# Widening of all MLP weights beside the expert tiles, and three pieces of them split there

## The chip, the cores and the metric

The kernel runs on one core of a Trainium2 chip. The metric is the device time of one execution in microseconds; before the change the median of three runs is 971.08 us (969.3 to 971.67).

## The reference, cut to what matters

Three layers follow each other on 2304 tokens (4 batches of 576) of 512 columns:

```python
# 1. attention per batch and head (D = 64), mixed with a memory read-out by a gate g
out = g * mem_out + (1 - g) * softmax(causal(q @ k.T / 8)) @ v
# 2. a mixture of 8 experts, one per token
e = argmax(x @ w_gate);  p = softmax(x @ w_gate)[e]
x = p * (relu(x @ w1[e]) @ w2[e])             # w1: 512 x 1024, w2: 1024 x 512
# 3. an MLP with an ELU, 512 -> 2048 -> 512
h = x @ w_in
y = where(h > 0, h, exp(min(h, 0)) - 1) @ w_out
```

`w_in` and `w_out` reach the kernel as 64-bit floats, all else as 32-bit floats.

## The kernel before, in words

**Matmuls.** A product of two float32 matrices is made of three passes of 128 x 128 x 512 in a reduced 32-bit format: each operand is split into a high part (a cast) and a low part (the operand less its high part), and high x high, low x high and high x low are added in PSUM. So each weight needs one cast (ScalarE or VectorE) and one subtraction (VectorE or GpSimd) before its first use; `split` records both.

**Stages.** Attention runs in pairs of heads. Then come 23 expert tiles of 128 tokens (tile 0 to 22), sorted by expert; two more tiles stand behind a branch that all engines take on a count made on the chip (`tc.If(nt > NTM)`), and are skipped when 23 suffice, as here. A tile loads its expert's weights (2 x 2 MB) only if the expert differs from the tile before, and splits them only then, in eight quarters: `w0` to `w3` (first matrix) and `w4` to `w7` (second). Even tiles load into `wraw`, odd ones into `wrbw`. A tile's second product is summed in one PSUM bank, `pm7`, which all tiles share, and evacuated from there into `y`.

**The MLP** takes the tokens in groups of 512 in the order of the expert tiles. A group has 16 units: 12 matmuls per 512 tokens for 128 columns of `w_in` (`h`), the ELU (ScalarE: `elu`, `tnh`; VectorE: three instructions), the split of the result (`gh`, `gl`), and 12 matmuls with `w_out`. The first group's tokens come from the first four tiles: two stay on the chip (`raw1n`), two are read back from `ye`; the tokens of later groups are scattered to `yd` and read from there.

**Its weights** are cut into 16 pieces of 512 KB, piece n = 2s + k: part k (0 `w_in`, 1 `w_out`) of slice s. Two things happen to a piece. *Widening* (class `Widen`) turns 64-bit words into 32-bit floats with integer operations, in two parts of 512 columns: a load of 512 KB into one of two buffers `wide`, one `Abs` on ScalarE, four VectorE instructions in `half`, and a store of 256 KB to `wf` in DRAM. Pieces 0 to 11 (24 parts) are widened beside the expert tiles. *Splitting* comes later: the piece is loaded back from `wf` and split into its place. Piece 0 is split beside the tiles; pieces 1 to 11 are loaded through `half`, `half1` and `wide` and split in the MLP's own program (`weights`); pieces 12 to 15 are widened there as well and split straight away. `raw0n` is piece 0, `wraw1n`, `wraw2n`, `wraw3n` are pieces 1 to 3 (each lies over one of tile 22's buffers of raw weights, `wraw1` to `wraw3`), `w02` is piece 4, `w12` piece 5, `w03` piece 6.

**The order of the work** is made ahead of time: class `Plan` takes every operation with a cost, a priority and its reads and writes, simulates the engines, and emits them in order of their planned start. Each engine runs its own list strictly in that order, and so does SP, which issues nearly all loads and stores: an instruction that waits holds all behind it. An operation may name two engines, and the planner gives it to the one that is done first by its costs. Some operations of the MLP's plan (in the old program the splits of pieces 1 and 2, and loads into `wide` and `half`) stand ahead of the branch in the engines' lists.

Of the kernel before, what the change touches and what calls it, by code (L numbers as in the profile page):

```python
# [9 lines left out]
F32 = mybir.dt.float32  # L10
F32R = mybir.dt.float32r
# [7 lines left out]
P = 128  # L19
# [17 lines left out]
NY = 2  # L37
YW = NY * P

NS = 6  # L40
assert NE <= -(-((B - 1) * S - E * (P - 1)) // P)
BIG = 1.0e30
LATE = 25000.0
# [40 lines left out]
class Plan:  # L84
# [137 lines left out]


KNOBS = {
    "xe": ("ACT", "DVE"), "he": ("ACT",), "re": [("ACT",), ("ACT", "DVE")], "m_ld": 4000.0, "m_x": -2208.9, "m_1": -1447.9, "m_h": -4434.5,
    "m_lag": 0.0, "m_if": 700.0, "m_fl": -3000.0, "m_wl": 300.0, "wa": 0, "wa0": 10022.449169040721, "wa1": 23927.854833523612, "wt": 1, "wp": 16, "wj": 2000.0,
    "m_g": -500, "wq": 0.85, "sa": 60.0, "sm": 50.0, "s2": 0.0, "step": -68438.62, "hd": -241.62,
    "mem": 379947.52, "xg": 4,
    "wh": [("ACT", "DVE"), ("ACT", "DVE"), ("ACT", "DVE"), ("DVE",), ("ACT",), ("ACT", "DVE"), ("ACT", "DVE"), ("ACT", "DVE")],
    "wl": [("DVE",)] * 8, "ord": [3, 4, 2, 1, 0], "rings": 4, "ab": 2, "nq": 2, "nv": 2, "na": 2, "na4": 2, "nx": 2, "nls": 2, "wide": 1, "de": ("DVE", "POOL"),  # L230
# [224 lines left out]
def cv(n):  # L455
    return 70 + 1.04 * n
# [10 lines left out]
def cpt(n):  # L467
    return 150 + 2.1 * n
# [615 lines left out]
class Widen:  # L1084
# [3 lines left out]
    N = 512  # L1088
# [11 lines left out]
    def inside(cls, tc, c, w_in, w_out):  # L1100
        return cls(tc, c, w_in, w_out, cls.ring(c), Ring("wo", [c.half[:, cls.N * i:cls.N * (i + 1)] for i in range(2)]))

    def part(self, n, pr, to=None, **kw):
        nc, c, pl, N = self.nc, self.c, self.c.pl, self.N
        ch, hf = divmod(n, 2)
        k, s = ch % 2, ch // 2
        sd = Slot(self.words)
        so = to or Slot(self.out)

        def o():  # L1110
            return so.t[:, N * hf:N * (hf + 1)] if to else so.t

        def u():
            return o().bitcast(U32)

        def f():
            if k == 0:
                nc.sync.dma_start(sd.t.rearrange("p (c f) w -> p c (f w)", c=2), self.vi[s, :, 2 * hf:2 * hf + 2].rearrange("p c f w -> p c (f w)"))
            else:
                nc.sync.dma_start(sd.t, self.vo[s, :, hf])  # L1120
        pl.op("SP", 480, f, w=[sd], prio=pr, dma=1456, lag=c.K["m_wl"], **kw)
        w = [(so, hf)]

        def f():
            nc.scalar.activation(o(), sd.t[:, :, 1].bitcast(F32), AF.Abs)
        pl.op("ACT", ca(N, sb=True), f, r=[sd], w=w, prio=pr)

        def f():
            nc.vector.tensor_scalar(o(), o(), 2.0 ** -15, MAXHI, op0=ALU.max, op1=ALU.min)  # L1129
        pl.op("DVE", cv2(N), f, w=w, prio=pr)  # L1130

        def f():
            nc.vector.tensor_scalar(u(), u(), 5, 2, op0=ALU.logical_shift_left, op1=ALU.logical_shift_right)  # L1133
        pl.op("DVE", cv2(N), f, w=w, prio=pr)

        def f():
            nc.vector.scalar_tensor_tensor(u(), sd.t[:, :, 0], 29, u(), op0=ALU.logical_shift_right, op1=ALU.bitwise_or)  # L1137
        pl.op("DVE", cv(N), f, r=[sd], w=w, prio=pr)

        def f():  # L1140
            nc.vector.scalar_tensor_tensor(u(), sd.t[:, :, 1], 0xC0000000, u(), op0=ALU.bitwise_and, op1=ALU.bitwise_or)  # L1141
        pl.op("DVE", cv(N), f, r=[sd], w=w, prio=pr)
        if to:
            return

        def f():
            nc.sync.dma_start(c.wf[ch, :, N * hf:N * (hf + 1)], o())
        pl.op("SP", 480, f, r=w, w=[], prio=pr, dma=728, lag=c.K["m_wl"])
# [75 lines left out]
def moe(tc, c, w1, w2, tiles):  # L1224
    nc = tc.nc
    mp, pl, K = c.mp, c.pl, c.K
# [201 lines left out]
        mtile(t)  # L1428
    if tiles[0] == 0:

        sr = Slot(c.wd.words)

        def src():
            return sr.t.rearrange("p n w -> p (n w)").bitcast(F32)

        def f():
            nc.sync.dma_start(src(), c.wf[0])
        pl.op("SP", 480, f, r=[("tile", K["wp"]), "y0"], w=[sr], prio=1.0e6, dma=1456)
        split(c, src, lambda: c.w0.t[:, 0], lambda: c.w0.t[:, 1], 1024, [sr], "w0h", "w0", 1.0e6, False, ("ACT", "DVE"), ("DVE", "POOL"))


def moe2(tc, c, w_in, w_out, out):
    nc = tc.nc
    tp, pl = c.tp, c.pl
# [19 lines left out]
    def chunk(t, cc, n):  # L1464
# [19 lines left out]
    def split(src, hi, lo, n, rd, wh, wl, pr, psum, also=()):  # L1484
        def ha():
            nc.scalar.copy(hi(), src())  # L1486

        def hv():
            nc.vector.tensor_copy(hi(), src())  # L1489

        def lv():
            nc.vector.tensor_sub(lo(), src(), hi().bitcast(F32))  # L1492

        def lp():
            nc.gpsimd.tensor_sub(lo(), src(), hi().bitcast(F32))  # L1495
        pl.op(("ACT", "DVE"), (ca(n, sb=not psum), cv(n) if psum else cv2(n)), (ha, hv), r=rd, w=[wh, *also], prio=pr)
        if psum:
            pl.op("DVE", cv(n), lv, r=rd + [wh], w=[wl], prio=pr)
        else:
            pl.op(("DVE", "POOL"), (cv(n), cpt(n)), (lv, lp), r=rd + [wh], w=[wl], prio=pr)  # L1500

    def weights(s):
        for k in range(2) if s else (1,):
            def mk(k):
                pr = 200.0 * s + 50 * k
                sr = Slot(r_raw) if s > 1 else Slot(wd.words)
                rd = [(sr, 0), (sr, 1)] + (["raw"] if s > 1 else [])

                def src():
                    return sr.t if s > 1 else sr.t.rearrange("p n w -> p (n w)").bitcast(F32)  # L1510

                def f():
                    nc.sync.dma_start(src(), c.wf[2 * s + k])
# [5 lines left out]
                split(src, lambda: wpart(k, 0, s), lambda: wpart(k, 1, s), 1024, rd, ("w", k, 0, s), ("w", k, 1, s), pr - 1000, False)
            mk(k)  # L1520

    for s in range(8):
        weights(s)
# [10 lines left out]
    def prep(g):  # L1534
        pr = start[g] - 900
# [120 lines left out]
def kernel(ctx, tc, q, k, v, M_prev, z_prev, beta, w_gate, w1, w2, w_in, w_out, out):  # L1656
    nc = tc.nc
# [126 lines left out]
```

## Time and profile before

| | |
|---|---|
| median of three runs | 971.08 us |
| the profiled execution | 969.31 us, span 967.6 us |
| TensorE busy / VectorE / ScalarE / GpSimd | 930.2 / 642.6 / 439.8 / 187.2 us |
| mean granted clock of TensorE | 0.989 |
| moved by DMA | 105.79 MB |

The stages in that span: attention to some 260 us, expert tiles to 542 us (a tile every 12.4 us), the MLP to the end. A line of a timeline gives the start, the busy time, the engine, the source line, the operation and its tiles (out<-in), and in square brackets the idle time of the engine just before it and what ended that.

### The profile page before, as it was taken

The page shows a single profiled execution, that of the slowest core. Times are in us where ns is not written, and L with a number is a line of the kernel's source. Part 1 is how long each engine was busy: PE and PEld are TensorE (multiplying, and loading weights), DVE is VectorE, ACT ScalarE, POOL GpSimd, SP SyncE. Part 2 cuts the span into 40 slices and gives each one's busy share as a digit, 9 for nine tenths or more (in the row PEclk, how much of TensorE's full clock was granted, in tenths as well). Part 3 has the DMA queues.
Part 4 walks back from the last instruction along what each step waited for, and adds up shares of the span by engine and source line. Part 5 has one row for each costly group of instructions (what it writes and reads, how often), then busy time and mean ns, then how long its engine had stood idle before and what let it go on. Part 6 is the DMA issues. An engine that isn't in the chain of part 4 may idle for free. (4 is left out here: it accounts for less than half of the span.)

```text
span 967.6 us, 18413 instructions
## 1 busy us (share of the span) xinstructions
PE 930.2 (96%) x6858; PEld 768.9 (79%) x6858; DVE 642.6 (66%) x1183; ACT 439.8 (45%) x893; POOL 187.2 (19%) x249
## 2 busy tenths in 40 slices
PE   9998999989999999999999898999999999999996
PEld 6777777777688888888887787888888888888895
DVE  3888878797865478438896499754565556555553
ACT  4777778865643357347665344222122212222221
POOL 3443443443200112212210113010001000100010
PEclk8999999999999999999999899999999999999998
DMA  6323334261814685398875434110011000100000
GB/s 122 87 65 102 74 75 112 57 211 58 297 48 139 218 282 196 103 306 327 299 272 197 153 123 125 45 44 1 1 44 44 1 12 23 44 0 1 12 33 22
DMA packets 94867, 105.79 MB, mean 109 GB/s; under 512 B 64687, under 2 KB 64687, under 8 KB 92465
## 3 DMA queue, kind: packets, MB, share of 16 engines
q1 hardware_dynamic: 88768, 91.06, 30.4%
q0 software_dynamic: 4800, 13.18, 3.8%
q8 instruction: 55, 0.90, 0.4%
q10 hardware_dynamic: 1200, 0.30, 0.2%
q14 instruction: 44, 0.35, 0.1%
HBM read 85.84 MB, written 21.31 MB: 111 GB/s over the span
## 5 line engine op out<-in xcount | busy, mean ns | idle before, releaser
L1598 ACT ACTIVATE elu<-pt 128x512 f32<-128x512 f32 x72 | 43.1, 599 | 253.9 <-PE pt L1590 253.8
L1623 PE MATMUL pt<-w,gh 128*128 128x512 f32 x432 | 135.5, 395 | 0.5 <-DVE gh L1489 0.5
L1380 PE MATMUL pm<-w,hh 128*128 128x512 f32 x368 | 128.3, 410 | 2.9 <-ACT y L1393 2.9
L1606 DVE TENSOR_SCALAR elu<-elu 128x512 f32<-128x512 f32 x72 | 30.6, 427 | 119.8 <-ACT elu L1598 119.8
L1623 PEld LDWEIGHTS pt<-w,gh 128*128 128x128 f32 x432 | 80.3, 190 | 17.3 <-DVE gh L1489 0.9
L1623 PE MATMUL pt<-w,gl 128*128 128x512 f32 x216 | 85.7, 397 | 3.0 <-POOL gl L1495 3.0
L690 ACT ACTIVATE a<-pat,st 128x128 f32<-128x128 f32 (+2 forms) x144 | 78.2, 552 | 22.5 <-DVE st L685 21.4
L1380 PEld LDWEIGHTS pm<-w,hh 128*128 128x128 f32 x368 | 70.6, 192 | 18.7 <-ACT y L1393 3.4
L1380 PE MATMUL pm<-w,hl 128*128 128x512 f32 x184 | 74.3, 404 | 0.3 <-DVE hl L1214 0.3
L685 DVE TENSOR_REDUCE st<-pat 128x2 f32<-128x256 f32 (+4 forms) x80 | 63.8, 807 | 9.0 <-PE pat L669 9.0
L1590 PE MATMUL pt<-yTh,w 128*128 128x256 f32 (+1 forms) x288 | 68.6, 318 | 0.0
L703 PE MATMUL pat<-ident,a 128*128 128x128 f32 x400 | 55.0, 280 | 9.1 <-ACT a L690 8.8
L626 POOL TENSOR_SCALAR ex<-ex 128x512 f32<-128x512 f32 (+1 forms) x32 | 37.9, 1184 | 128.8 <-ACT ex L602 118.1
L703 PEld LDWEIGHTS pat<-ident,a 128*128 128x128 f32 x400 | 42.9, 141 | 16.8 <-ACT a L690 15.7
L1610 DVE SCALAR_TENSOR_TENSOR tnh<-tnh,elu 128x512 f32<-128x512 f32 x72 | 49.6, 690 | 5.8
L1337 PE MATMUL pm<-w,x 128*128 128x512 f32 x216 | 52.0, 392 | 1.3 <-DVE w L1214 0.9
L1590 PEld LDWEIGHTS pt<-yTh,w 128*128 128x128 f32 x288 | 48.6, 189 | 4.5
L1623 PEld LDWEIGHTS pt<-w,gl 128*128 128x128 f32 x216 | 40.9, 190 | 13.9 <-POOL gl L1495 3.9
L1614 DVE SCALAR_TENSOR_TENSOR tnh<-pt,tnh 128x512 f32<-128x512 f32 x72 | 49.7, 690 | 2.9
L1214 DVE TENSOR_TENSOR hl<-pm,hh 128x512 fp32r<-128x512 f32 x46 | 31.5, 687 | 29.8 <-ACTq L1311 18.1
L1492 DVE TENSOR_TENSOR gl<-tnh,gh 128x512 fp32r<-128x512 f32 x67 | 46.2, 690 | 4.1
L1337 PEld LDWEIGHTS pm<-w,x 128*128 128x128 f32 x216 | 40.2, 188 | 10.4 <-DVE w L1214 1.4
(343 smaller groups left out, 2116.7 us busy)
## 6 DMA issues: line engine op xcount, KB each, us to landing
wraw<-in_moe_w_dram SPq DMA_DIRECT2D x24, 1024.0 KB, 7.9
wrbw<-in_moe_w_dram SPq DMA_DIRECT2D x12, 1024.0 KB, 7.9
wide<-in_moe_w_in_dram SPq DMA_DIRECT2D x16, 512.0 KB, 6.0
wide<-in_moe_w_out_dram SPq DMA_DIRECT2D x16, 512.0 KB, 12.4
wf<-half SPq DMA_DIRECT2D x24, 256.0 KB, 3.1
q<-in_q_dram SPq DMA_DIRECT2D x32, 128.0 KB, 2.5
v<-in_v_dram SPq DMA_DIRECT2D x32, 128.0 KB
half<-wf SPq DMA_DIRECT2D x8, 512.0 KB, 6.9
```

The source lines that it names most:

```text
L626: nc.gpsimd.tensor_scalar(e, e, 1.0, 0.0, op0=ALU.min, op1=ALU.add)
L685: nc.vector.tensor_reduce(ss.t[:, 2 * i:2 * i + (2 if i < 4 else 1)], src(), axis=AX.X if i < 4 else AX.XY, op=ALU.min)
L690: nc.scalar.activation(sa[i].t[:, h, :] if i < 4 else sa[4].t[:, 0:S].rearrange("p (y n) -> p y n", y=2), src()[:, h, :] if i < 4 else src ...
L703: nc.tensor.transpose(w.t[:, y:y + P], t[:, j * P:(j + 1) * P], c.ident)
L1337: nc.tensor.matmul(g[hf].t, a.t[:, cc, :], b[:, 512 * hf:512 * (hf + 1)], start=(cc == 0 and n == 0), stop=(cc == 3 and n == 2))
L1380: nc.tensor.matmul(y.t, a.t[:, 2 * (q % 2) + jj, :], b[:, 512 * jj:512 * (jj + 1)], start=(q == 0 and jj == 0 and n == 0), stop=(q == 3 an ...
L1492: nc.vector.tensor_sub(lo(), src(), hi().bitcast(F32))
L1590: nc.tensor.matmul(h.t[:, n * j + n0:n * j + n1], w(cc, a, ft), b(cc), start=(cc == 0 and x == 0), stop=(cc == 3 and x == 2))
L1598: nc.scalar.activation(se.t, h.t, AF.Exp)
L1610: nc.vector.scalar_tensor_tensor(st.t, st.t, 0.0, se.t, op0=ALU.min, op1=ALU.mult)
L1614: nc.vector.scalar_tensor_tensor(st.t, h.t, 0.0, st.t, op0=ALU.max, op1=ALU.add)
L1623: nc.tensor.matmul(acc[a].t, y.t[:, n * j + P * a:n * j + P * (a + 1)], wsub(1, k, ft // 2)[:, ft % 2, :], start=(ft == 0 and x == 0), sto ...
```

## The change

All 16 pieces are widened beside the expert tiles (`NS` 8), so 32 parts instead of 24, one for each 0.64 of a tile instead of 0.85 (`wq`). Pieces 0, 1 and 2 are loaded back and split in the expert stage's plan, casts on ScalarE and subtractions on VectorE; pieces 1 and 2 may be loaded when the part of tile 22's raw weights that they replace has been read. In the MLP every piece from 3 on is loaded with one DMA into a ring of four buffers (`half1`, `half`, both `wide`), and split with a priority nearer to its use (250 instead of 1000 ahead). No subtraction of the MLP may go to GpSimd any more. The planner's cost of loading an expert's weights is 3500 instead of 4000, and that of the two `ye` loads 0.

```diff
-NS = 6
+NS = 8
-    ... "m_ld": 4000.0, ... "wq": 0.85, ...
+    ... "m_ld": 3500.0, ... "wq": 0.64, ...
 def moe(...):
-        sr = Slot(c.wd.words)
-        def src():
-            return sr.t.rearrange("p n w -> p (n w)").bitcast(F32)
-        def f():
-            nc.sync.dma_start(src(), c.wf[0])
-        pl.op("SP", 480, f, r=[("tile", K["wp"]), "y0"], w=[sr], prio=1.0e6, dma=1456)
-        split(c, src, lambda: c.w0.t[:, 0], lambda: c.w0.t[:, 1], 1024, [sr], "w0h", "w0", 1.0e6, False, ("ACT", "DVE"), ("DVE", "POOL"))
+        def first(i):
+            sr = Slot(c.wd.words)
+            def src():
+                return sr.t.rearrange("p n w -> p (n w)").bitcast(F32)
+            def f():
+                nc.sync.dma_start(src(), c.wf[i])
+            pr = 1.0e6 + i
+            pl.op("SP", 480, f, r=[("tile", K["wp"]), "y0"], w=[sr, *([("raw", 0, i)] if i else [])], prio=pr, dma=1456)
+            split(c, src, lambda: c.w0[i].t[:, 0], lambda: c.w0[i].t[:, 1], 1024, [sr], ("w0h", i), ("w0", i), pr, False, ("ACT",), ("DVE",))
+        for i in range(3):
+            first(i)
 def moe2(...):
-    r_raw = Ring("raw", [c.half, second])
-    wd = Widen(tc, c, w_in, w_out, Widen.ring(c), None)
+    r_raw = Ring("raw", [second, c.half, *c.wide])
     def split(src, hi, lo, n, rd, wh, wl, pr, psum, also=()):
-        if psum:
-            pl.op("DVE", cv(n), lv, r=rd + [wh], w=[wl], prio=pr)
-        else:
-            pl.op(("DVE", "POOL"), (cv(n), cpt(n)), (lv, lp), r=rd + [wh], w=[wl], prio=pr)
+        pl.op("DVE", cv(n), lv, r=rd + [wh], w=[wl], prio=pr)
-    def weights(s):
-        for k in range(2) if s else (1,):
-                if s < NS:
-                    pl.op("SP", 480, f, w=rd[0:2] + ([] if s > 1 else [("raw", s, k)]), prio=pr - (3000 if s < 2 else 2000), dma=1456)
-                else:
-                    for hf in range(2):
-                        wd.part(4 * s + 2 * k + hf, pr - c.K["wj"], sr, r=["raw"])
-                split(src, ..., rd, ("w", k, 0, s), ("w", k, 1, s), pr - 1000, False)
+    def weights(s, k):
+        pr = 200.0 * s + 50 * k
+        sr = Slot(r_raw)
+        def f():
+            nc.sync.dma_start(sr.t, c.wf[2 * s + k])
+        pl.op("SP", 480, f, w=[sr], prio=pr - 2000, dma=1456)
+        split(lambda: sr.t, ..., [sr, "raw"], ("w", k, 0, s), ("w", k, 1, s), pr - 250, False)
+    for n in range(3, 16):
+        weights(*divmod(n, 2))
-                pl.op("SP", 480, f, w=[sy], prio=pr - 1500 + a, dma=728)
+                pl.op("SP", 480 if g else 0, f, w=[sy], prio=pr - 1500 + a, dma=728 if g else 0)
```

ScalarE's list where the second matrix of tile 21 ends and that of tile 22 begins, before (`y1` is tile 21's evacuation, `wraw0` under L1393 tile 22's):

```order
L1313 CAST w50_3735<-wraw2_75 128x1024
L1311 UNCONDITIONAL_BRANCH x2
L1316 UNCONDITIONAL_BRANCH
L1486 CAST wraw2n_7177<-wide1_70 128x1024
L1393 ACTIVATE y1_3748<-pm7_3719,xg0_3728 128x512
L1311 COMPARE_AND_BRANCH
L1313 CAST w60_3733<-wraw3_76 128x1024
L1313 CAST w70_3731<-wraw3_76 128x1024
L1311 UNCONDITIONAL_BRANCH x2
L1316 UNCONDITIONAL_BRANCH
L1393 ACTIVATE wraw0_73<-pm7_3719,xg1_3729 128x512
```

and now, at the same place (L1391 is the evacuation, L1206 the cast of the new splits):

```order
L1311 CAST w50_3735<-wraw2_75 128x1024
L1309 UNCONDITIONAL_BRANCH x2
L1314 UNCONDITIONAL_BRANCH
L1391 ACTIVATE y1_3748<-pm7_3719,xg0_3728 128x512
L1309 COMPARE_AND_BRANCH
L1311 CAST w60_3733<-wraw3_76 128x1024
L1311 CAST w70_3731<-wraw3_76 128x1024
L1309 UNCONDITIONAL_BRANCH x2
L1314 UNCONDITIONAL_BRANCH
L1206 CAST wraw2n_6882<-wide0_69 128x1024
L1391 ACTIVATE wraw0_73<-pm7_3719,xg1_3729 128x512
```

The cast into `wraw2n` has moved from ahead of the evacuation of `y1` to behind the casts of `w6` and `w7`.

SP's list, the first loads behind the branch, before; ahead of the branch stand loads of pieces 1, 2 and 4 (into `wide0`, `wide1` and `half`):

```order
L1513 DMA half1_7115<-wf_63 128x1024
L1547 DMA wraw0_73<-yd_62 128x516
L1513 DMA wide0_69<-wf_63 128x1024
L1547 DMA wraw0_73<-yd_62 128x516 x2
L1118 DMA wide1_70<-in_moe2_w_in_dram 128x2x512
L1513 DMA half_71<-wf_63 128x1024
```

and now; ahead of the branch stand loads of pieces 1 and 2 only:

```order
L1505 DMA half1_7179<-wf_63 128x1024
L1505 DMA half_71<-wf_63 128x1024
L1505 DMA wide0_69<-wf_63 128x1024
L1505 DMA wide1_70<-wf_63 128x1024
L1534 DMA wraw0_73<-yd_62 128x516 x3
L1505 DMA half1_7179<-wf_63 128x1024
```

Pieces 3 to 6 are now loaded in a row, ahead of the first rows of `yd`, and no piece is loaded at the branch.

ScalarE's list behind the branch, before (`yTh` is the split of the tokens read back from `ye`, `elu` and `tnh` the activations of the first units):

```order
L1486 CAST yTh_7116<-pt2_7109 128x4x128
L1486 CAST w02_7129<-half_71 128x1024
L1486 CAST w12_7135<-half1_7115 128x1024
L1598 ACTIVATE elu0_7119<-pt0_7107 128x512
L1602 ACTIVATE tnh0_7121<-pt0_7107 128x512
```

and now:

```order
L1487 CAST yTh_7180<-pt1_7172 128x4x128
L1487 CAST w02_7193<-half_71 128x1024
L1586 ACTIVATE elu0_7183<-pt0_7171 128x512
L1590 ACTIVATE tnh0_7185<-pt0_7171 128x512
L1586 ACTIVATE elu1_7184<-pt2_7173 128x512
```

One cast (piece 4, `w02`) stands ahead of the activations instead of two, but its piece is now loaded behind the branch.

## Rows read from the trace of the kernel before

**Rows 1.** Busy time by stage: stretch, length, PE, PEld, DVE, ACT, POOL, clock, DMA share, GB/s:

```profile
410.00:500.00 90.00, 90.00 (x438) 74.63 (x436) 67.08 (x88) 55.43 (x77) 17.59 (x22) 1.00 0.91 317
445.00:520.00 75.00, 74.51 (x360) 61.65 (x359) 67.82 (x85) 52.14 (x70) 13.50 (x18) 1.00 0.82 286
260.00:500.00 240.00, 238.82 (x1187) 197.78 (x1185) 158.33 (x246) 128.90 (x189) 42.56 (x50) 1.00 0.66 225
500.00:542.00 42.00, 38.58 (x166) 30.89 (x165) 27.40 (x33) 20.53 (x28) 3.94 (x7) 0.92 0.40 139
542.00:612.00 70.00, 64.07 (x410) 56.95 (x410) 58.59 (x96) 28.55 (x47) 13.42 (x8) 0.98 0.42 136
```

**Rows 2.** Waits of PE, 260 to 543 us: total, times, longest:

```profile
PE pm L1380 <- ACT y L1393: 2.9, 1, 2.9
...
PE pm L1362 <- DVE h L1350: 0.5, 1, 0.5
```

**Rows 3.** Timeline of PE, last tiles and branch:

```profile
530.14 0.40 PE L1380 MATMUL pm<-w,hh 128*128 128x512 f32 x1
533.48 0.79 PE L1380 MATMUL pm<-w,hh 128*128 128x512 f32 x1 [2.93 <-ACT y L1393]
...
540.95 0.63 PE L1380 MATMUL pm<-w,hh 128*128 128x512 f32 x2
...
541.65 0.40 PE L1380 MATMUL pm<-w,hh 128*128 128x512 f32 x1
542.87 3.14 PE L1590 MATMUL pt<-raw1n,raw0n 128*128 128x256 f32 x24 [0.82 <-ACTq L1744]
545.85 1.03 PE L1558 MATMUL pt<-ident,wraw 128*128 128x128 f32 x8
```

**Rows 4.** Timeline of DVE and ACT, around the gap at 530 us:

```profile
529.35 2.36 DVE L1318 TENSOR_TENSOR w<-wraw,w 128x1024 fp32r<-128x1024 f32 x2 [0.25 <-ACT w L1313]
...
531.79 1.04 ACT L1486 CAST wraw2n<-wide 128x1024 fp32r<-128x1024 f32 x1 [1.52 <-issue]
532.74 0.68 ACT L1393 ACTIVATE y<-pm,xg 128x512 f32<-128x512 f32 x1
```

**Rows 5.** Waits of PE, 543 to 612 us:

```profile
PE pt L1623 <- POOL gl L1495: 3.0, 2, 2.6
...
PE pt L1590 <- ACTq L1744: 0.8, 1, 0.8
```

**Rows 6.** Timeline of POOL and PE, around the gap at 602 us:

```profile
600.27 4.00 POOL L1495 TENSOR_TENSOR gl<-tnh,gh 128x512 fp32r<-128x512 f32 x1 [7.33 <-ACT gh L1486]
...
604.32 0.80 PE L1623 MATMUL pt<-w,gl 128*128 128x512 f32 x1 [2.57 <-POOL gl L1495]
...
608.28 1.55 PE L1590 MATMUL pt<-raw1n,w 128*128 128x256 f32 x12
```

**Rows 7.** Instructions on tile half: duration min/median/max in ns:

```profile
L1125 ACT ACTIVATE half<-wide x32: 656/676/702, 288.6 to 604.8; 128x512 f32<-128x512 f32 x32
L1129 DVE TENSOR_SCALAR half<-half x32: 412/422/679, 289.3 to 606.6; 128x512 f32<-128x512 f32 x32
...
L1137 DVE SCALAR_TENSOR_TENSOR half<-wide,half x32: 679/692/721, 292.0 to 608.2; 128x512 uint32<-128x512 uint32 x32
...
L1492 DVE TENSOR_TENSOR w<-half,w x12: 1212/1218/2299, 548.7 to 613.4; 128x1024 fp32r<-128x1024 f32 x12
```

**Rows 8.** Timeline of SP, the first load behind the branch:

```profile
542.89 0.32 SPq L1513 DMA_DIRECT2D half<-wf  x1
```

**Rows 9.** Busy time and DMA after that load, columns as in rows 1:

```profile
546.50:547.00 0.50, 0.39 (x4) 0.14 (x2) 0.00 (x0) 0.39 (x1) 0.00 (x0) 1.00 0.01 0
```

**Rows 10.** DMA issues, 260 to 545 us: number, KB each, us to landing:

```profile
wide<-in_moe_w_out_dram SPq DMA_DIRECT2D x12, 512.0 KB, 12.4
...
yd<-y,r_pos POOLq DMA_INDIRECT x18, 5.6
...
yd<-wraw,r_pos POOLq DMA_INDIRECT x1, 3.9
```

More of the change, by code (lines that the diff above doesn't have):

```diff
@@ L224 @@
 KNOBS = {
-    "xe": ("ACT", "DVE"), "he": ("ACT",), "re": [("ACT",), ("ACT", "DVE")], "m_ld": 4000.0, "m_x": -2208.9, "m_1": -1447.9, "m_h": -4434.5,
+    "xe": ("ACT", "DVE"), "he": ("ACT",), "re": [("ACT",), ("ACT", "DVE")], "m_ld": 3500.0, "m_x": -2208.9, "m_1": -1447.9, "m_h": -4434.5,
     "m_lag": 0.0, "m_if": 700.0, "m_fl": -3000.0, "m_wl": 300.0, "wa": 0, "wa0": 10022.449169040721, "wa1": 23927.854833523612, "wt": 1, "wp": 16, "wj": 2000.0,
-    "m_g": -500, "wq": 0.85, "sa": 60.0, "sm": 50.0, "s2": 0.0, "step": -68438.62, "hd": -241.62,
+    "m_g": -500, "wq": 0.64, "sa": 60.0, "sm": 50.0, "s2": 0.0, "step": -68438.62, "hd": -241.62,
     "mem": 379947.52, "xg": 4,
@@ L1101, in inside, with part @@
         return cls(tc, c, w_in, w_out, cls.ring(c), Ring("wo", [c.half[:, cls.N * i:cls.N * (i + 1)] for i in range(2)]))
-    def part(self, n, pr, to=None, **kw):
+    def part(self, n, pr, **kw):
         nc, c, pl, N = self.nc, self.c, self.c.pl, self.N
@@ L1107, in part @@
         sd = Slot(self.words)
-        so = to or Slot(self.out)
+        so = Slot(self.out)
         def o():
-            return so.t[:, N * hf:N * (hf + 1)] if to else so.t
+            return so.t
         def u():
@@ L1470, in moe2 @@
     r_o = Ring("osb", [Later(last, None, i, None) for i in range(4)])
-    W = [[tp.tile([P, 2, 1024], F32R, name=f"w{k}{s}") if s > 1 else Later(c.wp, f"wraw{2 * s + k}", [P, 2, 1024], F32R) if s + k else c.w0
+    W = [[tp.tile([P, 2, 1024], F32R, name=f"w{k}{s}") if s > 1 else c.w0[2 * s + k]
           for s in range(8)] for k in range(2)]
@@ L1496, in split @@
         pl.op(("ACT", "DVE"), (ca(n, sb=not psum), cv(n) if psum else cv2(n)), (ha, hv), r=rd, w=[wh, *also], prio=pr)
-        if psum:
-            pl.op("DVE", cv(n), lv, r=rd + [wh], w=[wl], prio=pr)
-        else:
-            pl.op(("DVE", "POOL"), (cv(n), cpt(n)), (lv, lp), r=rd + [wh], w=[wl], prio=pr)
-    def weights(s):
-        for k in range(2) if s else (1,):
[L1504 to L1513, printed above, removed]
-                if s < NS:
-                    pl.op("SP", 480, f, w=rd[0:2] + ([] if s > 1 else [("raw", s, k)]), prio=pr - (3000 if s < 2 else 2000), dma=1456)
-                else:
-                    for hf in range(2):
-                        wd.part(4 * s + 2 * k + hf, pr - c.K["wj"], sr, r=["raw"])
[L1519 to L1523, printed above, removed]
+        pl.op("DVE", cv(n), lv, r=rd + [wh], w=[wl], prio=pr)
[5 more added lines that the diff above has]
+        pl.op("SP", 480, f, w=[sr], prio=pr - 2000, dma=1456)
+        split(lambda: sr.t, lambda: wpart(k, 0, s), lambda: wpart(k, 1, s), 1024, [sr, "raw"], ("w", k, 0, s), ("w", k, 1, s), pr - 250, False)
+    for n in range(3, 16):
+        weights(*divmod(n, 2))
     sizes = [512] * (NTOK // 512) + [NTOK % 512] * (NTOK % 512 > 0)
@@ L1688 @@
     c.ex = wp.tile([P, QW], F32, name="ex")
-    c.w0, c.y0 = [Later(wp, f"raw{i}", [P, 2, 1024], F32R) for i in range(2)]
+    c.w0 = [Later(wp, f"wraw{i}" if i else "raw0", [P, 2, 1024], F32R) for i in range(4)]
+    c.y0 = Later(wp, "raw1", [P, 2, 1024], F32R)
     nx = 3 * XW
```

2 lines of the change are left out of this document (removed).

## Prediction

> **What bounds the kernel now.** I read the page first: TensorE is the busiest engine by far, in nearly every slice. So only time in which it stands still, or runs at its lower clock, can be won: the change issues the same 6023 matmul instructions, in nearly the same order. The second view, busy time by stage, says where such time is [rows 1]. The expert stage (260 to 500 us) holds 1.2 us of idle in 240; the stretch that ends it (500 to 542) 3.4 us in 42 at a mean clock of 0.92; the first 70 us of the MLP 5.9 us at 0.98. Third come the waits of TensorE, and the timeline where each stands.
>
> At 530.54 us (530.14 + 0.40) TensorE ends the second matrix of tile 21 and starts tile 22 at 533.48, 2.93 us later, for ScalarE's evacuation of `y`, which has one PSUM bank [rows 2, 3]. ScalarE had not begun it: ahead in its queue stood the cast into `wraw2n`, the first half of the split of an MLP piece. It lies over `wraw2`, which VectorE read until 531.71 (529.35 + 2.36), so the cast started at 531.79 and the evacuation at 532.74 [rows 4]. After the gap the clock is at its lower level, 1.2 GHz, for some microseconds: the tile's 24 matmuls, 533.48 to 542.05, take 8.57 us, 0.36 each, while the three from 540.95 to 541.65 take 0.233 each, the upper level, 2.4 GHz [rows 3].
>
> At 601.7 the same happens for 2.57 us. There TensorE waits for a subtraction `gl` given to GpSimd, which took 4.00 us [rows 5, 6]; ten matmuls behind it take 3.96 us instead of 2.33.
>
> **The change part by part.** The profiled execution took 969.31 us, with a span of 967.6 and 1.7 us around it; the sum is made against it. The median of the three runs, 971.08, is 1.77 above it.
>
> *Tile 21 to 22.* In the new order of ScalarE the evacuation stands ahead of the last two casts of expert weights, and the cast into `wraw2n` behind both. What is late next is the evacuation itself, since TensorE has no other work between the two groups: 0.68 us with 0.05 us on either side, as at 533.42 to 533.48, so 0.8 us of the gap stays. A gap of 0.82 us (542.05 to 542.87) leaves the clock alone: the next 24 matmuls of half the width take 2.98 us to 545.85, 0.12 each [rows 3]. Before, 530.54 to 542.05 took 11.51 us; now 0.8 + 24 x 0.233 + 0.17 for the last one's tail = 6.55. Gain 4.95 us. The splits that tile 22 still needs do not come late: two casts from 531.4 on, the first subtraction a microsecond behind the first cast and 1.2 us long, so 533.7, where TensorE asks for it at 534.6.
>
> *Start of the MLP.* From 542 to 612 the idle time is 5.93 us [rows 1]. The 0.8 us at the branch stays [rows 5]; 5.11 can go, and with them 3.96 - 2.33 = 1.63 us of lower clock, in all 6.74. No subtraction goes to GpSimd any more (five of `gl` did). Eight widening parts leave this stretch, each four VectorE instructions of 0.42, 0.43, 0.69 and 0.69 us = 2.2 us and 0.68 us of ScalarE [rows 7]: 17.8 us of VectorE's 58.6.
>
> What comes new: no load is under way at the branch. Take T as TensorE's start behind it (before: 542.87; the new load of `half1` was issued at 542.89 and had landed by 546.5, T + 3.6 [rows 8, 9]). Now four loads of 512 KB go out in a row, piece 3 to 6. A piece is 0.524 MB, and the transfer engines moved 317 GB/s at a busy share of 0.91 [rows 1], so 348 GB/s full: 1.5 us each. Piece 4 has landed at about T + 5.1 to 5.9. On ScalarE its cast stands ahead of the activations of the first two units, on VectorE the split of piece 3 and the subtraction of piece 4 do, so all these wait: its cast, 1.04 us [rows 4], to T + 6.2 to 7.0; VectorE's subtraction, 1.22 [rows 7], to 7.4 to 8.2, and then five instructions of 0.42 to 0.69 us, some of them waiting for the activations, 2.5 to 2.9 in all, to 9.9 to 11.1. TensorE has work until T + 10: 72 matmuls at 0.12 (8.7 us) and twelve transposes (eight took 1.03 [rows 3]). Then it wants the bank that the fifth of those frees, so the new wait is 0 to 1.1 us.
>
> Just before that, four transposes need the first row block of `yd`, which is loaded once the scatter of tile 22 has landed; that took 3.9 us with one load beside it, and 5.6 us at the median of 18 [rows 10]. The scatter starts at T + 0.7, the `yd` loads go out at T + 4.6 to 6.3, behind piece 6 on their queue, and land by T + 9 to 9.7, where TensorE asks at T + 9.5. By the Trainium skill (page DMA: Bandwidth & Descriptors, section Queues, rings and completion order) each transfer engine takes turns between the queues it has work for, packet by packet; the scatter has a queue of its own, so by it the four loads slow the scatter but do not go ahead of it, which agrees with 5.6 us and gives the times above. By one line for all queues the scatter would land behind 2.4 MB, near T + 8, and the transposes would wait some 2 us more. I keep 1.0 us for both new waits together (0 to 3). Gain 6.74 - 1.0 = 5.75 us.
>
> *The expert stage.* The eight parts, and the loads and splits of pieces 1 and 2, now stand between the tiles, a part each 0.64 tile (8 us) instead of 0.85. TensorE is the bound there, so what they add is hidden as long as no queue is full. VectorE is nearest to that from 445 to 520, where five of the 7 tiles bring new experts: 67.8 us busy of 75 with 7 parts [rows 1]. The new order has 9 there: + 4.4 - 0.7 (the cast of piece 0 is ScalarE's now) = 71.5 of 75. The transfer engines are nearest from 410 to 500: 0.91 of 90 us. Three more parts, each 512 KB read and 256 KB written, 0.79 MB, are 2.36 MB or 6.8 us: 88.7 of 90. Both fit, barely. What the bound of one part is: a part's buffer is used again 16 us later, and the slowest such load took 12.4 us [rows 10]. Of what waits if it is late: ScalarE's `Abs` stands at the head of its queue, behind it the relu of the next tile, and for that TensorE. Bounds: - 0.5 us (the one gap there, 0.49 us at 500 for VectorE's relu [rows 2], comes where the old order has two parts in one tile; the new has one) to 5 us, one gap like that at 530. I take 0.5 us of cost net, nearer to the low end, since ScalarE and VectorE idle several microseconds in each tile without new weights.
>
> *The rest.* The knob for the loads' cost and the zero cost of the two `ye` loads only move loads whose data has 10 us or more to spare: 0. Attention and the later MLP keep their order: 0.
>
> Sum: 4.95 + 5.75 - 0.5 = 10.2 us; 969.31 - 10.2 = 959.1 for an execution like the profiled one, 960.9 from the median. I say **960.0 us**.
>
> **Rivals.**
> 1. *The loads behind the branch come too late.* For it: nothing is loaded ahead any more, and two queues stop on it. If the new wait is over 2.5 us the clock falls as at 601.7, so 2.57 + 1.63 = 4.2 us come back: 964.5. Against it: the first load landed at T + 3.6.
> 2. *Slower: ScalarE's queue stops on part loads in the expert stage.* Place: the 30 parts from tile 5 on; it decides where loads of 4 MB of expert weights fill the line ahead of a part. Price: a stop that leaves TensorE idle as at 530 costs 2.1 us more than the 0.8 and 2.8 of lower clock, 4.95. Two stops eat the gain; three give 971.08 - 10.2 + 15 = 976. For it: 88.7 of 90 us. Against it: in the old order no part's wait of ScalarE stopped TensorE, though one load took 12.4 us.
> 3. *The boundary of tiles 21 and 22 does not do what it says*, because something else (the subtractions, or `raw` pieces still being loaded) holds the evacuation: 4.95 us are lost again, 965. Against it: ScalarE is free at 530.3, before TensorE ends.
>
> **How the numbers follow.** Forecast 0.68, rival 1 0.12, rival 2 0.12 (three stops or more 0.08, fewer 0.04), rival 3 0.08 (0.02 of it with other losses). Own range of the forecast: the bounds of its two unknown terms are 0 to 3 for 1.0 and - 0.5 to 5 for 0.5; the best is 969.31 - 12.2 = 957.1, the worst likely, one end but not both, 971.08 - 5.7 = 965.4. To leave out no more than 2 in 10 I reach to rivals 1 and 3 and give it 956.5 to 967. A measurement of this kernel tells about 0.3%, 2.9 us, from no change: faster 0.68 + 0.12 + 0.06 = 0.86, same 0.04 + 0.02 = 0.06, slower 0.08.
>
> **What would show it.** Right: a gap of 0.8 us and no lower clock where the last tile begins; idle of 1 to 2.5 us in the 70 us behind the branch and no GpSimd subtraction; the expert stage as long as before within a microsecond, at clock 1.00. Wrong: ScalarE waiting for part loads with TensorE idle beside it, a gap over 2.5 us near T + 10, or VectorE without a pause from tile 15 on and the tiles more than 12.5 us apart.

## The result and the profile after

The changed kernel took 961.70 us (median of four runs, 957.23 to 962.65), the kernel before 970.55 us beside it: a ratio of 0.990, 95% interval 0.9866 to 0.9934. The forecast was 960.0. The profiled execution took 961.42 us with a span of 959.7; the one before took 969.31 with 967.6.

The two gaps that the prediction went for are gone. First busy time by stage of the changed kernel (stretch, length, PE, PEld, DVE, ACT, POOL, granted clock, DMA share, GB/s), against [rows 1]:

```profile
410.00:500.00 90.00, 89.87 (x433) 74.48 (x432) 66.73 (x91) 58.85 (x83) 21.92 (x23) 1.00 0.91 315
445.00:520.00 75.00, 74.62 (x360) 61.62 (x359) 66.35 (x88) 56.86 (x79) 17.08 (x18) 1.00 0.93 332
260.00:500.00 240.00, 238.69 (x1186) 197.84 (x1185) 166.57 (x274) 135.98 (x202) 46.69 (x49) 1.00 0.71 243
500.00:542.00 42.00, 40.51 (x190) 32.57 (x188) 31.54 (x38) 25.18 (x36) 6.40 (x9) 1.00 0.57 208
542.00:612.00 70.00, 69.22 (x459) 63.28 (x460) 50.99 (x81) 28.55 (x46) 3.08 (x6) 1.00 0.38 124
```

The clock from 500 to 542 us is 1.00 instead of 0.92, and the 70 us behind the branch hold 0.8 us of idle instead of 5.9. Next TensorE's timeline at the last tile and the branch, against [rows 3]:

```profile
534.49 0.40 PE L1378 MATMUL pm<-w,hh 128*128 128x512 f32 x1
535.67 0.50 PE L1378 MATMUL pm<-w,hh 128*128 128x512 f32 x1 [0.78 <-ACT y L1391]
...
541.14 0.40 PE L1378 MATMUL pm<-w,hh 128*128 128x512 f32 x1
542.36 1.69 PE L1578 MATMUL pt<-raw1n,raw0n 128*128 128x256 f32 x12 [0.82 <-ACTq L1733]
```

And ScalarE's timeline there, against [rows 4]:

```profile
534.93 0.69 ACT L1391 ACTIVATE y<-pm,xg 128x512 f32<-128x512 f32 x1 [0.31 <-PE pm L1378]
535.51 1.99 ACT L1311 CAST w<-wraw 128x1024 fp32r<-128x1024 f32 x2
537.40 1.04 ACT L1206 CAST wraw2n<-wide 128x1024 fp32r<-128x1024 f32 x1
```

ScalarE now stands ready 0.31 us before TensorE ends tile 21, and the cast into `wraw2n` comes behind. The gap of 0.78 us is the evacuation itself, and from the end of tile 21 (534.89) to that of tile 22 (541.54) it takes 6.65 us where it took 11.51.

But the branch stands at 542.36, only 0.51 us earlier than before. The loss lies ahead of all that the change touches. Busy time in one stretch of attention, the first profile of before, then after:

```profile
204.00:216.00 12.00, 11.64 (x195) 9.38 (x192) 11.07 (x43) 8.63 (x25) 5.92 (x7) 1.00 0.84 305
```

```profile
204.00:216.00 12.00, 11.87 (x141) 9.92 (x142) 8.79 (x39) 6.61 (x15) 3.59 (x3) 0.57 0.77 275
```

The matmuls are the same in both, and so are TensorE's waits just ahead of that stretch (0.66, 0.81, 0.21 and 0.48 us from 199 us on). Yet the mean granted clock is 0.57 after, so that some 10 of the 12 us are at 1.2 GHz, and 54 fewer matmuls fit in. The first expert matmul starts at 245.50 us instead of 241.29. So spans cannot be compared directly; the stages can. The expert stage is taken from that matmul to T (TensorE's start behind the branch), the MLP from T to the end of the span:

| kernel, profiled once each | first expert matmul | expert stage | MLP |
|---|---|---|---|
| before / again | 241.29 / 245.19 | 301.58 / 300.44 | 424.73 / 424.67 |
| changed / again | 245.50 / 242.95 | 296.86 / 298.02 | 417.34 / 417.33 |
| casts on VectorE | 245.43 | 297.10 | 423.97 |
| no GpSimd | 244.22 | 300.42 | 419.36 |
| widening moved | 244.30 | 300.28 | 429.72 |
| only piece 0 split early | 242.43 | 296.68 | 418.59 |
| GpSimd again | 243.46 | 298.40 | 422.14 |
| denser parts | 243.31 | 297.21 | 417.98 |
| load cost back | 242.75 | 300.06 | 436.09 |
| widening moved, cost 3500 | 243.31 | 300.89 | 420.30 |
| scatter early | 245.40 | 296.93 | 416.87 |
| denser and early | 243.22 | 297.28 | 418.60 |

By stages the change gives 4.72 + 7.39 = 12.1 us between the first two profiles, and attention takes 4.2 of it back.

### The profile page after: what moved, and what is told of

It is laid out like the page before. It is cut to its first block, busy times and chain, and to the rows that moved or that the text cites. A ratio compares the mean times of both kernels' runs of the same rounds, so it can differ in the third digit from the quotient of the medians.

```text
span 959.7 us, 18446 instructions
## 1 busy us (share of the span) xinstructions
PE 930.1 (97%) x6858; PEld 771.6 (80%) x6858; DVE 639.3 (67%) x1179; ACT 447.4 (47%) x902; POOL 181.5 (19%) x244
## 5 line engine op out<-in xcount | busy, mean ns | idle before, releaser
L1378 PE MATMUL pm<-w,hh 128*128 128x512 f32 x368 | 126.2, 404 | 0.8 <-ACT y L1391 0.8
L703 PE MATMUL pat<-ident,a 128*128 128x128 f32 x400 | 57.9, 290 | 8.6 <-ACT a L690 8.3
L703 PEld LDWEIGHTS pat<-ident,a 128*128 128x128 f32 x400 | 45.4, 147 | 16.1 <-ACT a L690 15.2
L1493 DVE TENSOR_TENSOR gl<-tnh,gh 128x512 fp32r<-128x512 f32 x72 | 49.6, 691 | 4.2
```

Of the source, the lines that this page charges most:

```text
L703: nc.tensor.transpose(w.t[:, y:y + P], t[:, j * P:(j + 1) * P], c.ident)
L1378: nc.tensor.matmul(y.t, a.t[:, 2 * (q % 2) + jj, :], b[:, 512 * jj:512 * (jj + 1)], start=(q == 0 and jj == 0 and n == 0), stop=(q == 3 an ...
```

## The experiments

**Both kernels once more.** No edit.

> The changed kernel as it is, for its time beside the next three and for a second profile. The first profile has a stretch from 204 to 214 us, inside attention, at the lower clock (mean granted clock 0.57 in 204 to 216, against 1.00 before), where both kernels issue the same instructions on TensorE and wait the same short times; everything behind it stands 4.2 us later (first expert matmul at 245.50 against 241.29). Theory A: that loss belongs to single executions, not to the change: some runs have it and some not, in both kernels, and a run without it takes 957 us with a mean clock of 0.995. Theory B: the change causes it, and then it stands in every run of the changed kernel, at 961 to 963 us and a clock of 0.987 to 0.990.

> The kernel before as it is, for a second profile of it. In three profiles of the changed kernel and its parts the stretch from 130 to 216 us ran with 1.6 to 4.2 us less work done than in the first profile of before, at a lower clock, with the same instructions. Theory A (that spell falls on either kernel in single executions): the first expert matmul comes between 242.5 and 245.5 us here too, the execution takes 970 to 974 us. Theory B (before does not have it): 241.3 us again and a time of 968.5 to 970.

The changed kernel took 961.57 us against 969.70 beside it, ratio 0.9919 (0.9903 to 0.9935). The kernel before took 972.05 us in its second profiled execution, and the same stretch now reads:

```profile
204.00:216.00 12.00, 11.87 (x139) 9.79 (x140) 8.77 (x38) 6.32 (x15) 3.97 (x5) 0.58 0.76 276
```

So the spell in attention falls on the kernel before too, and the changed kernel has it in different lengths (245.50, 242.95): theory A. Of all 14 profiles only the first of before starts the experts at 241.29; the others lie 1.1 to 4.2 us later. The prediction's sum was made against an execution that is unusual among these 14. What makes the spell long or short stays open, as does whether it is longer on average in one kernel.

**The tile boundary alone** (kernel before; the casts of pieces 1 and 2 go to VectorE):

```diff
+        if wh in (("w", 0, 0, 1), ("w", 1, 0, 0)):
+            pl.op("DVE", cv2(n), hv, r=rd, w=[wh, *also], prio=pr)
+        else:
+            pl.op(("ACT", "DVE"), ...)
```

> The kernel before, with the casts of pieces 1 and 2 on VectorE, so that ScalarE's evacuation of y of tile 21 has no cast into wraw2n ahead of it; nothing else changes. Theory A (the cast in ScalarE's queue is the cause of the 2.93 us gap, and the gap the cause of the lower clock): the gap is 0.8 us, no lower clock in 530 to 542, 4.3 to 5 us less than before, 965.5 to 966.3 us; VectorE's subtractions for tile 22 come 0.7 us later, which may leave 0.6 us of a new gap. Theory B (something else holds the evacuation, or the clock falls whatever the gap): gap over 2 us or a lower clock, 970 to 971 us.

967.33 us, ratio 0.9968 (0.9953 to 0.9982), 2.4 us less by medians; I had 965.5 to 966.3. The mechanism is theory A's: the clock from 530 to 542 us is 1.00, the expert stage takes 297.10, and the gap is

```profile
535.49 0.50 PE L1380 MATMUL pm<-w,hh 128*128 128x512 f32 x1 [0.78 <-ACT y L1393]
```

The size depends on the execution compared with: 4.5 us less than the first profile of before, 3.3 less than the second. Both have a gap of 2.9 us, but the lower clock that comes with it lasts for different times, by the means some 7 and some 3 of these 15 us. PE's busy time and clock, first profile, then second:

```profile
530.00:545.00 15.00, 11.24 (x44) 8.70 (x43) 5.29 (x5) 4.46 (x6) 2.46 (x3) 0.77 0.10 32
```

```profile
530.00:545.00 15.00, 11.87 (x44) 8.83 (x42) 7.09 (x7) 6.16 (x8) 1.48 (x2) 0.89 0.07 28
```

**No GpSimd in the MLP, alone** (kernel before):

```diff
-            pl.op(("DVE", "POOL"), (cv(n), cpt(n)), (lv, lp), r=rd + [wh], w=[wl], prio=pr)
+            pl.op("DVE", cv(n), lv, r=rd + [wh], w=[wl], prio=pr)
```

> The kernel before, with no subtraction of the MLP on GpSimd; the widening of pieces 12 to 15 stays in the MLP. Theory A (the 4.00 us subtraction on GpSimd at 600 us is the cause of the 2.57 us gap and of the 1.63 us at the lower clock behind it): 4 to 4.5 us less, 966 to 966.5 us. Theory B (VectorE, which keeps the 17.8 us of widening there, is late with these subtractions instead): a gap for VectorE at the same place, 969 to 971 us.

964.83 us, ratio 0.9949 (0.9931 to 0.9967). Theory A, and a little more: the MLP lost 5.37 us where the prediction had 2.57 + 1.63 = 4.2 for the stop at 602 us. TensorE waited for GpSimd twice there, 3.0 us in all [rows 5], and neither wait is left. The 2.93 us gap at the last tile stayed, as it should.

**The widening moved, alone** (kernel before):

```diff
-NS = 6
+NS = 8
-    "wq": 0.85
+    "wq": 0.64
```

> The kernel before, with all 32 parts beside the expert tiles, one for each 0.64 tile; pieces 1 and 2 are now loaded and split behind the branch, and GpSimd may still subtract. Theory A (the widening itself costs nothing in the expert stage, and what pays is that three split pieces stand ready at the branch): the gap at the last tile goes, 4.95 us less; but behind the branch TensorE has 24 matmuls of half width, 2.9 us, for the one piece that is ready, and stands 4 to 6 us until piece 2 has landed and is split, with a lower clock behind it: 968 to 972 us. Theory B (the parts in the MLP were what cost, and late pieces are hidden): 960 to 964 us.

975.28 us, ratio 1.0058 (1.0042 to 1.0074): slower, beyond what I expected. The waits of TensorE from 260 us:

```profile
PE pt L1558 <- DMA wraw<-ye: 6.8, 1, 6.8
PE pt L1590 <- ACTq L1744: 5.0, 1, 5.0
```

The gap at the last tile shrank to 0.97 us, as expected. But TensorE waited 5.0 us at the branch for ScalarE, and 6.8 us behind it for the load of `ye`. The last parts stood around the branch. Was it that, or pieces 1 and 2 behind it? The next three tell.

**Only piece 0 split beside the tiles** (changed kernel):

```diff
-        for i in range(3):
+        for i in range(1):
-    for n in range(3, 16):
+    for n in range(1, 16):
```

> The changed kernel with only piece 0 split beside the tiles; pieces 1 and 2 are loaded behind the branch too, ahead of piece 3. All else as changed: no widening in the MLP, no subtraction on GpSimd. Theory A (what the three split pieces do is give TensorE work until the first loads have landed and been split): TensorE has 24 to 48 matmuls of half width, 3 to 6 us, then stands until pieces 1 and 2 are split, some T + 8 to 9, and the clock falls behind it: 5 to 8 us more than the changed kernel, 967 to 970 us. Theory B (the gain of the MLP is from the widening and GpSimd alone): within 1.5 us of the changed kernel, 961 to 963 us.

963.05 us, ratio 0.9929 (0.9911 to 0.9946). Theory B, at its upper end; theory A fell: the MLP is 1.26 us longer, not 5 to 8. Piece 0 gives TensorE more than I counted (48 matmuls of half width and eight transposes), until T + 7.1, and it goes on with piece 2 without a wait. So the early pieces 1 and 2 gain little at the branch: the one wait that this run has more there is 0.7 us.

**The load cost alone undone** (changed kernel):

```diff
-    "m_ld": 3500.0
+    "m_ld": 4000.0
```

> The changed kernel with one number undone: the planner's cost of loading an expert's weights is 4000 again instead of 3500. In its order three stores and two loads of widening parts now stand on SP behind the branch, between piece 3 and piece 4. The prediction gave this number nothing. In the run with the widening alone moved (which has 4000 too) ScalarE came to the branch 5.0 us late behind such parts, and TensorE stood 6.8 us for a load of ye. Theory A (that number is what ends the parts before the branch, and so carries most of the MLP's gain): the MLP, from the branch to the end, takes 422 to 430 us instead of 417.3, and the execution 966 to 975 us. Theory B (the number moves only loads with time to spare, as predicted): MLP 417 to 418, 961 to 962 us.

981.13 us, ratio 1.0115 (1.0094 to 1.0135): 20 us slower than the changed kernel, and beyond both theories. SP's queue behind the branch (T is 542.81):

```profile
546.35 0.32 SPq L1505 DMA_DIRECT2D half<-wf  x1
546.72 0.42 SPq L1120 DMA_DIRECT2D wide<-in_moe_w_out_dram  x1
553.22 0.32 SPq L1145 DMA_DIRECT2D wf<-half  x1
553.58 0.43 SPq L1120 DMA_DIRECT2D wide<-in_moe_w_out_dram  x1
555.47 5.17 SPq L1145 DMA_DIRECT2D wf<-half  x2
562.37 0.32 SPq L1505 DMA_DIRECT2D half<-wf  x1
562.80 0.84 SPq L1505 DMA_DIRECT2D wide<-wf  x2
563.70 1.50 SPq L1534 DMA_DIRECT2D wraw<-yd  x3
```

and what TensorE waits for:

```profile
569.91 1.11 PE L1546 MATMUL pt<-ident,wraw 128*128 128x128 f32 x4 [15.76 <-DMA wraw<-yd]
```

Three stores of parts wait on SP for VectorE's work on these parts (12.3 us in all) and hold the queue until 560.6; the load of piece 4 goes out at 562.37, the `yd` loads at 563.70. One number of the planner moves the last parts from ahead of the branch to behind it.

**The widening moved, with that number** (kernel before, `NS` 8, `wq` 0.64):

```diff
-    "m_ld": 4000.0
+    "m_ld": 3500.0
```

> The kernel before with the widening alone moved, as in the run that took 975.28 us, and with the planner's cost of 3500 instead of 4000; pieces 1 and 2 behind the branch, GpSimd may subtract. Theory A (that run lost its time only by the parts that stood around the branch): its two stops of 5.0 and 6.8 us go; expert stage near 297 us, MLP 418 to 423 us by what GpSimd is given, 961 to 966 us. Theory B (the loss was from pieces 1 and 2): still 970 us or above.

966.87 us, ratio 0.9966 (0.9947 to 0.9984), 8.4 us less than with 4000. Both long stops are gone and the MLP takes 420.30. I was wrong on the expert stage: in this order the cast of piece 2 stands ahead of the evacuation again, the 2.9 us gap is back, and the stage takes 300.89. So the moved widening with the cost of 3500 pays by some 4.4 us in the MLP (424.73 to 420.30); with 4000 the parts end behind the branch and it does not pay. GpSimd still makes two `gl` here, in 1.35 and 1.81 us, and TensorE waits for neither: this edit removes the stop at 602 us too.

**GpSimd allowed again** (changed kernel; the edit of the run without GpSimd, reversed).

> The changed kernel, with the subtractions of the MLP allowed on GpSimd again; the planner then gives it four of the weights' (pieces 6, 8, 9 and 11), none of gl. Theory A (a subtraction on GpSimd costs only where TensorE waits for it soon; four of twice the size, some 8 us each, stand far ahead of their use except the first): 0 to 3 us more than the changed kernel, 961.5 to 965 us. Theory B (any use of GpSimd there brings back the stop of before): 4 us more or above, 966 us.

964.88 us, ratio 0.9942 (0.9921 to 0.9964). Within theory A by the time, but the MLP is 4.8 us longer, and not for the reason I gave: TensorE waits for VectorE, not for GpSimd. VectorE:

```profile
560.00 0.68 DVE L1605 SCALAR_TENSOR_TENSOR tnh<-pt,tnh 128x512 f32<-128x512 f32 x1
560.60 2.72 DVE L1601 SCALAR_TENSOR_TENSOR tnh<-tnh,elu 128x512 f32<-128x512 f32 x1
563.24 2.59 DVE L1490 CAST gh<-tnh 128x512 fp32r<-128x512 f32 x1
...
566.96 0.41 DVE L1490 CAST gh<-tnh 128x512 fp32r<-128x512 f32 x1
...
568.23 0.68 DVE L1601 SCALAR_TENSOR_TENSOR tnh<-tnh,elu 128x512 f32<-128x512 f32 x1
568.83 3.40 DVE L1493 TENSOR_TENSOR w<-wide,w 128x1024 fp32r<-128x1024 f32 x1
```

and GpSimd beside it:

```profile
560.37 2.41 POOL L1496 TENSOR_TENSOR w<-half,w 128x1024 fp32r<-128x1024 f32 x1 [1.18 <-ACT w L1487]
562.73 2.82 POOL L1496 TENSOR_TENSOR w<-wide,w 128x1024 fp32r<-128x1024 f32 x1
568.67 2.48 POOL L1496 TENSOR_TENSOR w<-half,w 128x1024 fp32r<-128x1024 f32 x1 [3.12 <-ACT w L1487]
```

Three VectorE instructions that meet a GpSimd subtraction end about their own length after it: 2.72 us instead of 0.68, 2.59 instead of 0.41, 3.40 instead of 1.22. TensorE then waits 1.46 us for `gh` and 0.46 us for `gl`, and its clock falls behind them; its wait, and its busy time and clock (columns as in the stages):

```profile
565.89 0.74 PE L1614 MATMUL pt<-wraw3n,gh 128*128 128x512 f32 x2 [1.46 <-DVE gh L1490]
```

```profile
568.00:571.00 3.00, 3.00 (x8) 2.30 (x7) 3.00 (x3) 2.49 (x3) 2.33 (x1) 0.50 0.05 21
```

The kernel before has such a meeting too, GpSimd and then VectorE:

```profile
559.19 1.29 POOL L1495 TENSOR_TENSOR gl<-tnh,gh 128x512 fp32r<-128x512 f32 x1 [4.79 <-DVE gh L1489]
```

```profile
559.44 2.12 DVE L1492 TENSOR_TENSOR w<-half,w 128x1024 fp32r<-128x1024 f32 x1 [0.34 <-ACT w L1486]
```

The Trainium skill (page SBUF — State Buffer, section SBUF: two separate sides) says that the two engines share one pair of ports, and that whichever starts first (on VectorE an instruction in a two-port mode or with two SBUF inputs) holds it to its end while the other blocks. These rows agree: each VectorE instruction ends 0.3 to 1.1 us, about its own length, behind the GpSimd one. It would also explain why the subtraction of `gl` took 1.29 us at 559.19, where GpSimd came first, and 4.00 us at 600 us [rows 6], where VectorE was busy without a pause; no run separated that.

**Denser parts** (changed kernel):

```diff
-    "wq": 0.64
+    "wq": 0.5
```

> The changed kernel, with a widening part for each half tile instead of each 0.64, so that the 32 parts are done by tile 17. In one of the two profiles of the changed kernel ScalarE stood 3.5 us for a part's load at 482.9 to 486.4 us, and the evacuation of h behind it left TensorE idle for 1.41 us. Theory A (rival 2: a part load that lands late stops ScalarE's queue and with it TensorE, and closer parts bring more of it): one to four more such stops of 0.5 to 1.5 us each between 380 and 480 us, no lower clock behind a stop of that length; 962 to 966 us. Theory B (there is room for them, since the transfer engines are at 0.70 over the stage): 961 to 962 us, the stops at most as long as in the changed kernel.

960.49 us, ratio 0.9902 (0.9885 to 0.992): theory B, half a microsecond below it. Its only stop for ScalarE's `h` is 0.8 us. The stop that led to this run, ScalarE in the second profile of the changed kernel:

```profile
482.21 0.69 ACT L1391 ACTIVATE y<-pm,xg 128x512 f32<-128x512 f32 x1 [2.16 <-PE pm L1378]
486.45 0.66 ACT L1125 ACTIVATE half<-wide 128x512 f32<-128x512 f32 x1 [3.55 <-DMA wide<-in_moe_w_out_dram]
487.01 1.04 ACT L1311 CAST wq<-wraw 128x1024 fp32r<-128x1024 f32 x1
487.95 1.04 ACT L1311 CAST w<-wraw 128x1024 fp32r<-128x1024 f32 x1
488.89 1.07 ACT L1345 ACTIVATE h<-pm 128x512 f32<-128x512 f32 x2
```

The part's load lands late, two casts and `h` queue up behind it, and TensorE stands for 1.41 us:

```profile
489.54 0.66 PE L1360 MATMUL pm<-ident,h 128*128 128x128 f32 x4 [1.41 <-ACT h L1345]
```

In the first profile of the changed kernel there is a stop of 0.2 us only.

**Scatter early** (changed kernel; the first `yd` load goes ahead of pieces 5 and 6 on SP):

```diff
-... prio=pr - 1500 + a, ...
+... prio=pr - 1500 + a - (1226 if g == 1 else 0), ...
```

> The changed kernel with the load of the first row block of yd, which waits for the scatter of tile 22, ahead of the loads of pieces 5 and 6 on SP; nothing else differs on any engine. So two loads of 512 KB stand before the scatter instead of four. In the changed kernel the scatter landed 7.1 us after its issue, in the kernel before, with one load beside it, after 3.9 us. One line (the scatter lands behind all that was issued ahead of it): 1.5 us for each of the two loads less, 4 to 5.2 us. Turns by queue (the Trainium skill, page DMA: Bandwidth & Descriptors, section Queues, rings and completion order): the loads do not go ahead of it, so 7 us again, or whatever it is that held it. In both the loads of pieces 5 and 6 are issued some 5 us later, and rival 1 says what follows if the pieces come too late: stops of 1 to 4 us, 962 to 966 us; if they have time to spare, 961 to 962 us.

960.72 us, ratio 0.9887 (0.9869 to 0.9906). The scatter of tile 22 in the list of DMA issues (number, us to landing), changed kernel, then this one:

```profile
yd<-wraw,r_pos POOLq DMA_INDIRECT x1, 7.1
```

```profile
yd<-wraw,r_pos POOLq DMA_INDIRECT x1, 5.5
```

With one load beside it it took 3.9 us [rows 10], with two 5.5, with four 7.1; the second profiles of both kernels have 3.6 and 7.0. So the loads do delay it, by 0.8 to 1.6 us each, and 5.5 lies nearer to the 4 to 5.2 us of one line than to 7. The Trainium skill (page DMA: Bandwidth & Descriptors, section Queues, rings and completion order) has each transfer engine take turns between its queues, packet by packet; I had read that as loads that do not go ahead of the scatter. The numbers do not refute turns, since no run shows how long one turn of a load lasts. Pieces 5 and 6, issued 5.6 us later than in the changed kernel, stopped nobody.

**Denser and early together** (changed kernel; the two edits above).

> The changed kernel with a part for each half tile and the first load of yd ahead of pieces 5 and 6, the two edits that took 960.49 and 960.72 us alone beside 961.57 of the changed kernel. If both small gains are real and add (0.3 us at the branch from the earlier scatter, 0.5 us from fewer stops of ScalarE): expert stage near 297, MLP near 417, 959.5 to 960.5 us. If they were spread between runs (the changed kernel's own runs lie between 957.2 and 963.2): 960.5 to 962 us, not to be told from the changed kernel. The scatter lands 5.5 us after its issue again.

958.99 us (958.16 to 963.88), ratio 0.9893 (0.9875 to 0.9912). The lowest median of all, but its interval overlaps that of the changed kernel, and its stages (297.28 and 418.60) are no shorter. No gain is shown; its scatter took 5.3 us.

## Why the prediction was right, and where it was not

**Tile 21 to 22, 4.95 us.** Right: 11.51 us became 6.65, so 4.86, with the gap of 0.78 that was foreseen. In the second profile of before the same stretch takes 10.36 us, so the term is 3.7 to 4.9: the gap was the same in both, the length of the lower clock was not.

**Start of the MLP, 5.75 us.** Direction right, size too small: 7.39 us. Busy time and clock from T to the end, before, changed, and before without GpSimd:

```profile
542.87:967.60 424.73, 410.80 (x2080) 344.92 (x2080) 254.85 (x438) 106.19 (x193) 35.66 (x38) 0.99 0.13 41
```

```profile
542.36:959.70 417.34, 408.14 (x2080) 344.35 (x2080) 239.94 (x411) 103.90 (x185) 23.33 (x33) 0.99 0.11 38
```

```profile
544.64:964.00 419.36, 408.67 (x2080) 344.23 (x2080) 252.81 (x439) 110.28 (x197) 23.08 (x33) 1.00 0.12 41
```

With the same 2080 matmuls TensorE's idle time fell by 4.73 us and its busy time by 2.66; the sum had 5.11 - 1.0 = 4.11 and 1.63. In idle time the miss is the new waits, 1.0 in the sum and 0.28 measured, so the 70 us hold less idle than the 1 to 2.5 us I had said would show it. In busy time 2.13 us already come with taking GpSimd out alone, half a microsecond more than the ten matmuls that I had priced at the lower clock; which others got shorter was not traced. Taking GpSimd out was worth 5.37 us in all, and the widening moved with the cost of 3500 gave 4.4, so the two gains overlap. What is left for the parts and the early pieces beside GpSimd is some 2 us.

**The new waits.** The scatter's landing was the step that failed: the `yd` loads were to go out at T + 4.6 to 6.3 and went out at T + 7.8, as in the reading by one line, which had T + 8. SP's load, then TensorE's wait for it:

```profile
550.14 1.27 SPq L1534 DMA_DIRECT2D wraw<-yd  x3
```

```profile
552.79 0.66 PE L1546 MATMUL pt<-ident,wraw 128*128 128x128 f32 x4 [0.28 <-DMA wraw<-yd]
```

It cost only 0.28 us, since TensorE asked at T + 10.1 and the load took under 3 us. The other new wait, for the fifth VectorE instruction, did not come.

**The expert stage, cost 0.5.** Right: 4.72 us less in all, with 4.86 from the boundary, leaves 0.1; the second profile leaves 1.3, by the stop shown above. The working was off: VectorE was to be busy 71.5 of 75 us with 9 parts and was 66.4 with 10, below the 67.8 of before. The prediction had moved one cast to ScalarE; six instructions of VectorE there (two relus, four casts, 4.2 us) are ScalarE's now, which is busy 56.9 us instead of 52.1. The transfer engines stayed at a share of 0.91 over 410 to 500, with eleven parts instead of eight, where 88.7 of 90 us had been worked out. And the 12.4 us of [rows 10], which I took for the slowest load of a part, are the one length that the profile gives for the loads from `w_out` (shortest, median and longest alike), so slower ones may have gone unseen.

**The rest, 0.** Wrong in one line. I wrote that the knob for the loads' cost moves only loads with time to spare. With that number alone set back the kernel takes 981 us, some 20 more than the changed kernel, so the MLP's gain needs it. I had compared the order before and after as a whole, never with one number changed. The zero cost of the `ye` loads, the ring of four buffers and the nearer priority of the splits were not undone alone. Attention, also put at 0, cost the first pair of profiles 4.2 us, though not by the change. The 6023 matmul instructions of the prediction stand in no profile: TensorE's records are 6858 in both kernels, so that they are the same number holds.

**The rivals.** Rival 1 was wrong: the loads behind the branch cost 0.28 us, and two of them 5.6 us later still stop nobody. Its bound for the clock was too high: in the run with GpSimd again the clock fell behind stops of 1.46 and 0.46 us, not only of over 2.5. Rival 2 is real as a mechanism: ScalarE did stop on part loads with TensorE behind it. Its price was wrong: the longest stops are 0.2 and 1.4 us in its two profiles and 1.7 in the run with GpSimd again, at a clock of 1.00, instead of 2.1 + 2.8 us. Rival 3 was wrong for the change; the run with 3500 alone shows what it would have been.

**The sum.** 10.2 us foreseen; 9.8 to 12.1 by stages, whichever profile of before stands against whichever of the changed kernel, 8.85 and 8.13 by medians. In the profiles what differs beside the stages lies in attention; for the medians that is not shown. The forecast of 960.0 against 961.7 is close in part by luck: an MLP term that was 1.6 us too small stands against a profile of before whose attention was faster than in any other.

## What to carry to other kernels

Before summing against one profile, take a second one of the same kernel and compare by stages: here attention alone moved by 4 us between executions of identical work. A planner's cost belongs to the change like any line of code: rebuild the order with that number alone set back before pricing it at nothing. Where an engine is given work to relieve another, look at how long the other's instructions take beside it.

## What the runs showed of the hardware

- With the same gap of 2.9 us the lower clock lasted longer in one execution than in another (mean 0.77 and 0.89 over the same 15 us). Gaps of 1.41 and 1.74 us in the expert stage left the clock at 1.00, while gaps of 1.46 and 0.46 us, 0.74 us of matmuls apart, had a clock of 0.50 from 568 to 571 us behind them. In attention 1.2 GHz came in one execution and not in another with no wait above 0.81 us just ahead of it.
- A GpSimd subtraction under way held up VectorE to its end: a 0.41 us cast took 2.59 us beside one. Whether VectorE holds up GpSimd in the same way was not separated.
- A scatter issued with loads under way landed 3.9, 5.5 and 7.1 us after its issue with one, two and four loads of 512 KB beside it.
